# Loading w_in in two column parts between the loads of head pairs 4 and 5, holding later loads, and storing the last output in two parts

## The chip, the cores and the metric

The kernel runs on one core of a Trainium2 chip. The metric is the device time of the slowest (here the only) core in microseconds, the median of several executions. Before the change it is 290.6 us (four runs, 289.97 to 291.48). The profile shows one execution with a span of 289.0 us.

Engines in the profile: PE is TensorE, PEld its weight loads, DVE is VectorE, ACT is ScalarE, POOL is GpSimd. SPq is the queue of DMA instructions that SyncE issues.

## The reference

Block-sparse attention for 4 batches of 8 heads (768 positions, head size 64), followed by a two-matrix feed-forward layer over all 3072 tokens:

```python
# per head: scale, causal mask and a mask of at most 3 chosen key blocks of 64
k_rep = k.reshape(B, H, n_blocks, 64, D).mean(axis=3)
gate  = einsum('bhsd,bhnd->bhsn', q, k_rep)      # causal blocks only
mask  = own block, or among the 3 largest gates  # and causal by position
attn  = softmax(where(mask, 0.125 * q @ k.T, -1e9)) @ v
# all heads of a token side by side: x is [3072, 512]
h   = x @ w_in                                   # w_in  [512, 2048]
out = gelu_tanh(h) @ w_out                       # w_out [2048, 512]
```

## The kernel before

The work goes by *pairs* of heads: pair p = 4 * batch + number in the batch, 16 pairs in all. For a pair, k, q and v are loaded, k and q are turned (from pair 3 on by VectorE, 32 by 32 blocks), the gates and the mask are made ("pre"), then scores, exponentials, weighted values, normalisation and the turn of the result ("heads"). After four pairs, the batch goes through w_in (16 column blocks f of 128, with a GELU each) and w_out (6 row blocks).

A small scheduler in Python places every operation on its engines before anything is emitted. It knows estimated durations and priorities, and its result is the order of instructions *on each engine*. On the chip VectorE and ScalarE take their lists in that order, so an instruction that waits for data also delays all instructions behind it on that engine (below: 9.11 us on VectorE). The Trainium skill says so too ("Perfetto Trace Analysis", Tensor Engine Instruction): ScalarE, VectorE and GpSimd are "strict FIFO".

The parts that the change touches:

```python
    def load(p, key, at_least):
        ...
        def emit_t(_):                      # k and q from pair 3 on: four DMAs
            sd = io.tile([128, NC * 4, 32], FP32, tag=key, name=f"{key}_sd_{p}")
            for hh in range(2):
                for a in range(2):
                    nc.sync.dma_start(      # 128-byte runs
                        out=sd[64 * hh + 32 * a:64 * hh + 32 * a + 32],
                        in_=SRC[key][b, 2 * hp + hh].rearrange(
                            "(t i) (a j) -> a i t j", i=32, j=32)[a])
        ...
        go = add({SP: us}, emit_t if dve else emit,
                 [free_sd.get(...), at_least] + ..., prio=...)

    def load_w(name, dst, src, n, deps, prio):      # w_in, w_out: 2 MB in float16
        view = src.rearrange("(i p) f -> p i f", p=128)
        def emit(_):
            nc.gpsimd.dma_start(out=dst, in_=view)
        go = add({POOL: 1.3}, emit, deps, prio=prio)
        go = add({SP: 11.5}, lambda _: None, [go], prio=prio)   # plan only
        return add({"NONE": 0.0}, lambda _: None, [go], prio=prio, lag=1.9)

    # the scheduler's calls, in order (cut)
    for p in range(NPAIR):
        load(p, "k", None)
        load(p, "q", None)
        if p < HP:                                   # HP = 4
            ...
            if p == HP - 1:
                load(p, "v", None)
                w_ready["in"] = load_w("in", w_in16, moe_w_in, HP,
                                       [ld["q", p], ld["v", p]], 399)
        else:
            load(p, "v", None)
        pre(p)
        ...                                          # heads, w_out, s1(b), s2(b)

    # first feed-forward product: waits for all of w_in
    mm = add({PE: 0.324}, mm_e, [mm, xts[b][ci], exps[b][-1], w_ready["in"]], ...)
    # second: one [128, 512] output tile, one copy and one store per row block
    for ti in range(NC): ...
        def out_e(_, ti=ti):
            nc.sync.dma_start(out=out_rows[b * NC + ti], in_=T["osb", b, ti])
```

The softmax here doesn't subtract the row's maximum and nothing guards it: scores larger than these inputs give would overflow.

Of the kernel before, what the change touches and what calls it, by code (L numbers as in the profile page):

```python
# [8 lines left out]
FP32 = mybir.dt.float32  # L9
FP16 = mybir.dt.float16  # L10
# [23 lines left out]
class Plan:  # L34
# [13 lines left out]
    def add(self, *a, **kw):  # L48
        op = Op(*a, **kw)
        self.ops.append(op)  # L50
        return op
# [70 lines left out]
def kernel(  # L122
# [9 lines left out]
    nc = tc.nc  # L132
    B, H, S, D = q.shape
    NBLK = S // 64
    NC = S // 128
    DM = H * D
    DFF = moe_w_in.shape[1]
    NF = DFF // 128
    HP = H // 2
# [12 lines left out]
    hd = ctx.enter_context(tc.tile_pool(name="hd", bufs=3))  # L152
# [4 lines left out]
    obp = ctx.enter_context(tc.tile_pool(name="obp", bufs=3))  # L157
# [16 lines left out]
    w_in16 = persist.tile([128, HP, DFF], FP16)  # L174
    w_out16 = persist.tile([128, NF, DM], FP16)
# [13 lines left out]
    PE, ACT, DVE, POOL, SP = "PE", "ACT", "DVE", "POOL", "SP"  # L189
    add = plan.add  # L190
    T = {}

    def copy(eng, out, in_):
        if eng == ACT:
            nc.scalar.copy(out=out, in_=in_)
        elif eng == POOL:
            nc.gpsimd.tensor_copy(out=out, in_=in_)
        else:
            nc.vector.tensor_copy(out=out, in_=in_)
# [13 lines left out]
    def load(p, key, at_least):  # L213
        b, hp = divmod(p, HP)

        def emit(_):
            sd = (iov if key == "v" else io).tile(
                [128, NC, 2, 64], FP32, tag=key, name=f"{key}_sd_{p}")
            for hh in range(2):
                nc.sync.dma_start(  # L220
                    out=sd[:, :, hh, :],
                    in_=SRC[key][b, 2 * hp + hh].rearrange(
                        "(c p) d -> p c d", p=128))
            T[key, p] = sd
        def emit_t(_):
# [4 lines that stand above are left out]
                    nc.sync.dma_start(  # L230
# [3 lines that stand above are left out]
            T[key, p] = sd  # L234
        if p == 0 and key != "v":
            sd = T[key, p] = io.tile([128, NC, 2, 64], FP32, tag=key,
                                     name=f"{key}_sd_{p}")
            for a in range(2):
                def emit_h(_, a=a):
                    for hh in range(2):  # L240
                        nc.sync.dma_start(  # L241
                            out=sd[:, 3 * a:3 * a + 3, hh, :],
                            in_=SRC[key][b, 2 * hp + hh].rearrange(
                                "(a c p) d -> a p c d", p=128, c=3)[a])
                go = add({SP: 0.95}, emit_h, [], prio=-500)
                ld[key, p, a] = add({"NONE": 0.0}, lambda _: None, [go],
                                    prio=0, lag=1.9)
            went[key, p] = go
            return
        dve = key != "v" and by_dve(p)  # L250


        us = 2.75 if dve else 1.75
        go = add({SP: us}, emit_t if dve else emit,
                 [free_sd.get((key, p - (PV if key == "v" else PF))), at_least]
                 + ([went["k", p], went["q", p]] if key == "v" else []),
                 prio=1000 * (b - 1) + 580 + hp if b else 10 * p - 500)
        went[key, p] = go
        ld[key, p] = add({"NONE": 0.0}, lambda _: None, [go],
                         prio=1000 * b + hp, lag=1.9)  # L260
# [8 lines left out]
            [ld["v", p], old],  # L269
            prio=1000 * (b - 1) + 599 + hp if b else 100 * hp - 55)  # L270

    def load_w(name, dst, src, n, deps, prio):
        res = []
        view = src.rearrange("(i p) f -> p i f", p=128)

        def emit(_):
            nc.gpsimd.dma_start(out=dst, in_=view)
        go = add({POOL: 1.3}, emit, deps, prio=prio)

        go = add({SP: 11.5}, lambda _: None, [go], prio=prio)  # L280
        return add({"NONE": 0.0}, lambda _: None, [go], prio=prio, lag=1.9)


    c_E = {}
# [706 lines left out]
    def s1(b):  # L991
        for f in range(NF):
            mm = None
            for ci in range(HP):
                def mm_e(_, f=f, ci=ci):
                    hps = plan.buf["hps", b, f]
                    for (u, e) in ((0, 512), (512, S)):
                        nc.tensor.matmul(  # L998
                            hps[:, u:e],
                            w_in16[:, ci, f * 128:(f + 1) * 128],  # L1000
                            T["xT", b][:, ci, u:e],
                            start=(ci == 0), stop=(ci == HP - 1))
                mm = add({PE: 0.324}, mm_e,
                         [mm, xts[b][ci], exps[b][-1], w_ready["in"]],
                         1000 * b + 600 + f, takes=("wide", ("hps", b, f)))

            def ge_e(_, f=f):
                if ("gT", b) not in T:
                    T["gT", b] = gtp.tile([128, NF, S], FP16, tag="gT",
                                          name=f"gT_{b}")  # L1010
                nc.scalar.activation(  # L1011
                    out=T["gT", b][:, f, :],
                    in_=plan.buf["hps", b, f][:, 0:S],
                    func=AF.Gelu_apprx_tanh, bias=0.0, scale=1.0)
            gelus.setdefault(b, []).append(
                add({ACT: 0.7}, ge_e,
                    [mm, table(("gelu", b), exps[b], 1000 * b + 599)]
                    + s2_done.get(b - 2, []),
                    1000 * b + 600 + f, gives=[("hps", b, f)]))

    def s2(b):
        kind = "ops" if b < B - 1 else "tail"
        prev = None
        for ti in range(NC):
            mm = prev
            for f in range(NF):
                def mm_e(_, ti=ti, f=f):
                    nc.tensor.matmul(  # L1028
                        plan.buf["ops", b, ti],
                        T["gT", b][:, f, ti * 128:(ti + 1) * 128],  # L1030
                        w_out16[:, f, :],
                        start=(f == 0), stop=(f == NF - 1))
                mm = add({PE: 0.216}, mm_e,
                         [mm, gelus[b][f], w_ready["out"]],
                         1000 * b + 1580 + 0.1 * ti,
                         takes=(kind, ("ops", b, ti)))
            prev = mm

            def cp_e(eng, ti=ti):
                osb = obp.tile([128, DM], FP32, tag="osb", name=f"osb_{b}_{ti}")  # L1040
                T["osb", b, ti] = osb
                copy(eng, osb, plan.buf["ops", b, ti])
            cp = add({DVE: 0.6, ACT: 0.5}, cp_e, [mm], 1000 * b + 500,
                     gives=[("ops", b, ti)])

            def out_e(_, ti=ti):
                nc.sync.dma_start(out=out_rows[b * NC + ti],
                                  in_=T["osb", b, ti])
            add({SP: 0.9}, out_e, [cp], 1000 * b + 500)
            s2_done.setdefault(b, []).append(mm)  # L1050

# [14 lines left out]
                takes=("warm", ("warm", n)), gives=[("warm", n)])  # L1066
    consts()
    w_ready = {}
    for p in range(NPAIR):
        load(p, "k", None)  # L1070
        load(p, "q", None)
        if p < HP:
            if p:
                load(p - 1, "v", None)
                cast_v(p - 1, None)
            if p == HP - 1:
                load(p, "v", None)
                cast_v(p, None)
                w_ready["in"] = load_w("in", w_in16, moe_w_in, HP,
                                       [ld["q", p], ld["v", p]], 399)  # L1080
        else:
            load(p, "v", None)
            cast_v(p, last[p - NB]["v"])
        if p:
            pre(p)
        else:
            pre_first()
        if p < HP - 1:
            continue
        for x in range(HP) if p == HP - 1 else (p,):  # L1090
            (both_heads if x < HP else heads)(x)
        if p == HP - 1:
            w_ready["out"] = load_w("out", w_out16, moe_w_out, NF,
                                    [ld["v", 3], last[HP - 1]["n"]], 581)
        b, hp = divmod(p, HP)
        if hp == HP - 1:
            s1(b)
            s2(b)
# [35 lines left out]
```

## Time and profile before

| Part of the profiled run, 289.0 us | from to (us) |
|---|---|
| attention of batch 0 | 0 to 59.3 |
| w_in on batch 0 | 59.3 to 81.3 |
| w_out on batch 0, mixed with attention of batch 1 | 81.5 to 122.7 |
| end of w_in on batch 1 | 146.6 |
| last w_out matmul | 285.3 |

TensorE is busy 94% of the span. From the page of the kernel before, the 40 equal slices of 7.2 us; a digit is the busy share in tenths, and PEclk is the granted TensorE clock in tenths of full speed:

```profile
PE   7899952999999999999999979999999999999997
...
PEclk9999995899999999999999999999999999999999
```

Slices 6 and 7 (36 to 50 us) are the hole, and the clock falls just behind it. The table by stretch of the kernel before gives the numbers. A row is the stretch, its length, the busy time and count of each engine, then the clock, the DMA share and GB/s:

```profile
core 0: us, PE busy (x) PEld busy (x) DVE busy (x) ACT busy (x) POOL busy (x), PEclk, DMA share, GB/s
30.00:40.00 10.00, 9.94 (x137) 6.06 (x137) 6.06 (x22) 9.17 (x13) 5.20 (x12) 1.00 1.15 193
40.00:48.50 8.50, 0.04 (x1) 0.05 (x2) 1.72 (x4) 0.85 (x2) 0.09 (x1) 0.67 1.09 193
48.50:53.00 4.50, 4.50 (x42) 2.83 (x42) 2.83 (x8) 1.62 (x2) 0.02 (x1) 0.50 1.42 175
```

TensorE does nothing for 8.5 us and then works at half clock for 4.5 us. No engine computes in the hole, while the DMA column stays high. The Trainium skill ("TensorE: Matmul & The Clock Gate", Part 1) says that a TensorE left idle for a window of about 3.4 us falls to half clock and comes back after a busy window; here the clock is 0.50 after the gap, and 0.99 from 53.0 to 59.3 us.

Why it waits is read from the chain of waits of the kernel before (start, length, what). The chain is followed back from the last instruction, so each line was released by the one above it:

```profile
31.60 0.70 SPq L230
...
32.34 9.48 SPq L230
...
41.87 4.75 DMA k_sd_683<-in_k_dram
...
46.75 0.98 DVE kT_5_817 L403
...
47.84 0.57 DVE xn_755 L902
...
48.45 0.50 PE bank_91 L914 x3
```

And from VectorE's instructions in order of time (the brackets hold the idle time before, and what ended it):

```profile
36.68 0.96 DVE L403 STREAM_TRANSPOSE kT_4_803<-k_sd_516 128x768 f32<-128x768 f32 x1
46.75 0.98 DVE L403 STREAM_TRANSPOSE kT_5_817<-k_sd_683 128x768 f32<-128x768 f32 x1 [9.11 <-DMA k_sd_683<-in_k_dram]
47.65 0.16 DVE L901 RECIPROCAL zr_1_835<-bank_90 128x6 f32<-128x6 f32 x1
47.84 0.56 DVE L902 TENSOR_TENSOR xn_755<-bank_90,zr_1_835 128x384 f16<-128x384 f32 x1
```

This is the key reading. `kT_5` is the turn of pair 5's k, which belongs to batch 1; TensorE's first matmul that uses what is made of it (pair 5's gates) comes at 64.91 us. `zr_1` and `xn_755` normalise a pair of batch 0, and TensorE needs them now. They stand behind `kT_5` in VectorE's list, so they wait 9.1 us for a load that has nothing to do with them. The load is late because its third DMA issue took 9.48 us. At that time GpSimd's w_in transfer was under way: issued at 30.56 us, landed 14.3 us later.

### The profile page before, as it was taken

The page shows a single profiled execution, that of the slowest core. Times are in us where ns is not written, and L with a number is a line of the kernel's source. Part 1 is how long each engine was busy: PE and PEld are TensorE (multiplying, and loading weights), DVE is VectorE, ACT ScalarE, POOL GpSimd, SP SyncE. Part 2 cuts the span into 40 slices and gives each one's busy share as a digit, 9 for nine tenths or more (in the row PEclk, how much of TensorE's full clock was granted, in tenths as well). Part 3 has the DMA queues.
Part 4 walks back from the last instruction along what each step waited for, and adds up shares of the span by engine and source line. Part 5 has one row for each costly group of instructions (what it writes and reads, how often), then busy time and mean ns, then how long its engine had stood idle before and what let it go on. Part 6 is the DMA issues. An engine that isn't in the chain of part 4 may idle for free.

```text
span 289.0 us, 5917 instructions
## 1 busy us (share of the span) xinstructions
PE 272.6 (94%) x2304; PEld 166.7 (58%) x2304; DVE 138.7 (48%) x453; ACT 182.5 (63%) x241; POOL 46.5 (16%) x111
## 2 busy tenths in 40 slices
PE   7899952999999999999999979999999999999997
PEld 5676621756666656565656545666556644655443
DVE  6679625485628998389526991184013310000000
ACT  3568860575689998258689980176799932664111
POOL 5112420300012332000015530000034400000000
PEclk9999995899999999999999999999999999999999
DMA  5999999999805987999999921151011311000121
GB/s 135 228 156 150 190 214 174 142 186 200 130 0 119 140 147 143 214 186 152 169 145 196 134 72 73 74 71 23 0 39 30 92 41 71 36 2 0 73 75 73
DMA packets 133149, 32.44 MB, mean 112 GB/s; under 512 B 127489, under 2 KB 129537, under 8 KB 133121
## 3 DMA queue, kind: packets, MB, share of 16 engines
q1 hardware_dynamic: 130528, 27.87, 56.5%
q0 software_dynamic: 2592, 4.19, 8.1%
q8 instruction: 18, 0.29, 0.5%
q14 instruction: 11, 0.08, 0.1%
HBM read 27.26 MB, written 6.29 MB: 116 GB/s over the span
## 4 chain that ended last, share of the span: by engine, by line
PE 58%; DVE 14%; SPq 13%; DMA 6%; ACT 5%; issue 3%; DVEq 0%; ACTq 0%
PE wide_89 L998 11%; PE wide_88 L998 11%; SPq L230 10%; PE bank_90 L1028 6%; PE bank_91 L1028 5%; PE bank_93 L1028 4%; PE bank_92 L1028 4%; PE wide_88 L752 2%; DMA v_sd_1910<-in_v_dram 2%; PE wide_89 L752 2%; DMA k_sd_683<-in_k_dram 2%; SPq L220 1%; SPq L241 1%; DMA k_sd_205<-in_k_dram 1%; PE wide_89 L830 1%
## 5 line engine op out<-in xcount | busy, mean ns | idle before, releaser
L998 PEld LDWEIGHTS <-w_in_107 128*128 128x128 f16 x512 | 50.4, 103 | 30.2 <-issue 1.0
L1028 PEld LDWEIGHTS <-gT_3437 128*128 128x128 f16 x96 | 9.4, 98 | 11.2
L1063 PEld LDWEIGHTS <-zero 128*128 128x128 f16 x110 | 11.0, 111 | 5.6 <-issue 2.7
L1028 PEld LDWEIGHTS <-gT_2754 128*128 128x128 f16 x96 | 9.1, 97 | 8.2
L1028 PEld LDWEIGHTS <-gT_1940 128*128 128x128 f16 x96 | 9.1, 99 | 7.8
L1028 PEld LDWEIGHTS <-gT_1041 128*128 128x128 f16 x96 | 9.3, 103 | 6.2
L998 PE MATMUL wide_89<-xT_1480,w_in_107 128*128 128x512 f16 x64 | 12.5, 325 | 0.1
L998 PE MATMUL wide_89<-xT_2414,w_in_107 128*128 128x512 f16 x64 | 12.5, 325 | 0.0
L1028 PE MATMUL bank_90<-w_out_108,gT_1041 128*128 128x512 f16 x48 | 12.5, 379 | 0.0
L998 PE MATMUL wide_88<-xT_1480,w_in_107 128*128 128x512 f16 x64 | 12.2, 325 | 0.0
L998 PE MATMUL wide_88<-xT_2414,w_in_107 128*128 128x512 f16 x64 | 12.2, 325 | 0.0
L998 PE MATMUL wide_88<-xT_412,w_in_107 128*128 128x512 f16 x64 | 12.1, 325 | 0.0
L998 PE MATMUL wide_88<-xT_3104,w_in_107 128*128 128x512 f16 x64 | 12.0, 326 | 0.0
L998 PE MATMUL wide_89<-xT_412,w_in_107 128*128 128x512 f16 x64 | 11.8, 326 | 0.0
L998 PE MATMUL wide_89<-xT_3104,w_in_107 128*128 128x512 f16 x64 | 11.7, 326 | 0.0
L722 ACT ACT_TABLE_LOAD x8 | 10.3, 1283 | 0.9 <-PEq L1118 0.8
L1063 PE MATMUL bank_90<-zero 128*128 128x256 f16 x33 | 9.5, 294 | 1.1 <-DVE bmask L170 1.1
L1011 ACT ACTIVATE gT_1041<-wide_88 128x768 f16<-128x768 f32 x8 | 6.5, 811 | 5.1 <-PE wide_88 L998 5.1
L1028 PE MATMUL bank_92<-w_out_108,gT_2754 128*128 128x512 f16 x32 | 9.7, 380 | 0.0
L1011 ACT ACTIVATE gT_2754<-wide_88 128x768 f16<-128x768 f32 x8 | 6.5, 810 | 4.3 <-PE wide_88 L998 4.2
L1011 ACT ACTIVATE gT_1940<-wide_89 128x768 f16<-128x768 f32 x8 | 6.5, 811 | 4.0 <-PE wide_89 L998 3.9
L1011 ACT ACTIVATE gT_3437<-wide_89 128x768 f16<-128x768 f32 x8 | 6.5, 811 | 3.9 <-PE wide_89 L998 3.9
(937 smaller groups left out, 690.8 us busy)
## 6 DMA issues: line engine op xcount, KB each, us to landing
w_in_107<-in_moe_w_in_dram POOLq DMA_DIRECT2D x1, 2048.0 KB, 14.3
w_out_108<-in_moe_w_out_dram POOLq DMA_DIRECT2D x1, 2048.0 KB, 15.9
k_sd_133<-in_k_dram SPq DMA_DIRECT2D x4, 96.0 KB, 2.3
q_sd_134<-in_q_dram SPq DMA_DIRECT2D x4, 96.0 KB, 2.4
k_sd_205<-in_k_dram SPq DMA_DIRECT2D x2, 192.0 KB, 3.6
v_sd_221<-in_v_dram SPq DMA_DIRECT2D x2, 192.0 KB, 4.3
q_sd_245<-in_q_dram SPq DMA_DIRECT2D x2, 192.0 KB, 4.3
k_sd_272<-in_k_dram SPq DMA_DIRECT2D x2, 192.0 KB, 4.5
```

Source lines behind the costliest of these rows:

```text
L220: nc.sync.dma_start(out=sd[:, :, hh, :], in_=SRC[key][b, 2 * hp + hh].rearrange("(c p) d -> p c d", p=128))
L230: nc.sync.dma_start(out=sd[64 * hh + 32 * a:64 * hh + 32 * a + 32], in_=SRC[key][b, 2 * hp + hh].rearrange("(t i) (a j) -> a i t j", i=32, ...
L241: nc.sync.dma_start(out=sd[:, 3 * a:3 * a + 3, hh, :], in_=SRC[key][b, 2 * hp + hh].rearrange("(a c p) d -> a p c d", p=128, c=3)[a])
L722: nc.scalar.activation(out=t, in_=bmask[:, 0, 0:1], func=AF.Exp if key[0] == "exp" else AF.Gelu_apprx_tanh, bias=0.0, scale=1.0)
L752: nc.tensor.matmul(st[:, x:e], kT16[i][h][0:76, k0], qT16[i][h][0:76, q0], start=True, stop=True)
L830: nc.tensor.matmul(st[:, 512 * h + x + lo - q0:512 * h + x + w], (T["E2"][h] if mask else kT16[i][0])[r, j * 128:(j + 1) * 128], qT16[i][m ...
L998: nc.tensor.matmul(hps[:, u:e], w_in16[:, ci, f * 128:(f + 1) * 128], T["xT", b][:, ci, u:e], start=(ci == 0), stop=(ci == HP - 1))
L1011: nc.scalar.activation(out=T["gT", b][:, f, :], in_=plan.buf["hps", b, f][:, 0:S], func=AF.Gelu_apprx_tanh, bias=0.0, scale=1.0)
L1028: nc.tensor.matmul(plan.buf["ops", b, ti], T["gT", b][:, f, ti * 128:(ti + 1) * 128], w_out16[:, f, :], start=(f == 0), stop=(f == NF - 1))
L1063: nc.tensor.matmul(plan.buf["warm", n][:, 0:256], zero, z, start=True, stop=True)
```

## The change

The intent is to stop the batch-1 loads and w_in from getting in each other's way. The loads of pair 4 (k, q) go ahead of w_in. w_in comes in two column parts, so that the first product can start on the first. All later loads are held, in the plan and on the chip, until the first part is there; on the chip this is done by a tiny DMA on SyncE that reads one element of w_in. The last output row block is computed, copied and stored in two halves. The diff, cut:

```diff
-    def load_w(name, dst, src, n, deps, prio):
+    def load_w(dst, src, deps, prio, parts=1):
+        view = src.rearrange("(i p) f -> p i f", p=128)
+        n = view.shape[2] // parts
         res = []
+        for x in range(parts):
+            def emit(_, x=x):
+                nc.gpsimd.dma_start(out=dst[:, :, x * n:(x + 1) * n],
+                                    in_=view[:, :, x * n:(x + 1) * n])
+            go = add({POOL: 1.1}, emit, deps, prio=prio)
+            go = add({SP: 11.5 / parts}, lambda _: None, [go] + res[-1:], prio=prio)
+            res.append(go)
+        return [add({"NONE": 0.0}, lambda _: None, [go], prio=prio, lag=1.9)
+                for go in res]
+
+    def hold_loads(deps):
+        def emit(_):
+            t = hd.tile([128, 1], FP32, tag="tab", name="tab_hold")
+            nc.sync.dma_start(out=t[0:1].bitcast(FP16), in_=w_in16[0:1, 0, 0:2])
+        return add({SP: 0.05}, emit, deps, prio=-1000)
 ...
-                         [mm, xts[b][ci], exps[b][-1], w_ready["in"]],
+                         [mm, xts[b][ci], exps[b][-1], w_ready["in"][2 * f // NF]],
 ...
+        parts = [(ti, 0, DM) for ti in range(NC)]
+        if b == B - 1:                       # last output in two halves
+            parts[-1:] = [(NC - 1, x, x + DM // 2) for x in (0, DM // 2)]
 ...
     for p in range(NPAIR):
-        load(p, "k", None)
-        load(p, "q", None)
+        for key in "kq":
+            if p != HP:
+                load(p, key, held[0] if held else None)
 ...
-                w_ready["in"] = load_w("in", w_in16, moe_w_in, HP,
-                                       [ld["q", p], ld["v", p]], 399)
+                for key in "kq":
+                    load(HP, key, None)
+                w_ready["in"] = load_w(w_in16, moe_w_in,
+                                       [went["v", p], went["q", HP]], 399, 2)
+                held.append(hold_loads([w_ready["in"][0]]))
         else:
-            load(p, "v", None)
+            load(p, "v", held[0])
```

Because a scheduler decides the order, the diff does not show the main effect: in VectorE's new list, pair 5's turn comes after both normalisations of pair 3 and after pair 4's mask.

More of the change, by code (lines that the diff above doesn't have):

```diff
@@ L270, in cast_v @@
             prio=1000 * (b - 1) + 599 + hp if b else 100 * hp - 55)
-    def load_w(name, dst, src, n, deps, prio):
+    def load_w(dst, src, deps, prio, parts=1):
+        view = src.rearrange("(i p) f -> p i f", p=128)
+        n = view.shape[2] // parts
         res = []
-        view = src.rearrange("(i p) f -> p i f", p=128)
+        for x in range(parts):
[3 more added lines that the diff above has]
+            go = add({POOL: 1.1}, emit, deps, prio=prio)
+            go = add({SP: 11.5 / parts}, lambda _: None, [go] + res[-1:],
+                     prio=prio)
+            res.append(go)
+        return [add({"NONE": 0.0}, lambda _: None, [go], prio=prio, lag=1.9)
+                for go in res]
+    def hold_loads(deps):
         def emit(_):
-            nc.gpsimd.dma_start(out=dst, in_=view)
-        go = add({POOL: 1.3}, emit, deps, prio=prio)
-        go = add({SP: 11.5}, lambda _: None, [go], prio=prio)
-        return add({"NONE": 0.0}, lambda _: None, [go], prio=prio, lag=1.9)
+            t = hd.tile([128, 1], FP32, tag="tab", name="tab_hold")
+            nc.sync.dma_start(out=t[0:1].bitcast(FP16),
+                              in_=w_in16[0:1, 0, 0:2])
+        return add({SP: 0.05}, emit, deps, prio=-1000)
     c_E = {}
@@ L1023, in s2, with mm_e, cp_e, out_e @@
         prev = None
-        for ti in range(NC):
+        parts = [(ti, 0, DM) for ti in range(NC)]
+        if b == B - 1:
+            parts[-1:] = [(NC - 1, x, x + DM // 2) for x in (0, DM // 2)]
+        for n, (ti, x0, x1) in enumerate(parts):
             mm = prev
             for f in range(NF):
-                def mm_e(_, ti=ti, f=f):
+                def mm_e(_, n=n, ti=ti, x0=x0, x1=x1, f=f):
                     nc.tensor.matmul(
-                        plan.buf["ops", b, ti],
+                        plan.buf["ops", b, n][:, 0:x1 - x0],
                         T["gT", b][:, f, ti * 128:(ti + 1) * 128],
-                        w_out16[:, f, :],
+                        w_out16[:, f, x0:x1],
                         start=(f == 0), stop=(f == NF - 1))
-                mm = add({PE: 0.216}, mm_e,
-                         [mm, gelus[b][f], w_ready["out"]],
+                mm = add({PE: 0.216 * (x1 - x0) / 512}, mm_e,
+                         [mm, gelus[b][f], w_ready["out"][0]],
                          1000 * b + 1580 + 0.1 * ti,
-                         takes=(kind, ("ops", b, ti)))
+                         takes=(kind, ("ops", b, n)))
             prev = mm
-            def cp_e(eng, ti=ti):
-                osb = obp.tile([128, DM], FP32, tag="osb", name=f"osb_{b}_{ti}")
-                T["osb", b, ti] = osb
-                copy(eng, osb, plan.buf["ops", b, ti])
-            cp = add({DVE: 0.6, ACT: 0.5}, cp_e, [mm], 1000 * b + 500,
-                     gives=[("ops", b, ti)])
-            def out_e(_, ti=ti):
-                nc.sync.dma_start(out=out_rows[b * NC + ti],
-                                  in_=T["osb", b, ti])
+            def cp_e(eng, n=n, x0=x0, x1=x1):
+                osb = obp.tile([128, DM], FP32, tag="osb", name=f"osb_{b}_{n}")
+                T["osb", b, n] = osb
+                copy(eng, osb[:, x0:x1], plan.buf["ops", b, n][:, 0:x1 - x0])
+            cp = add({DVE: 0.6, ACT: 0.5} if x1 - x0 == DM else
+                     {DVE: 0.33, ACT: 0.36}, cp_e, [mm], 1000 * b + 500,
+                     gives=[("ops", b, n)])
+            def out_e(_, n=n, ti=ti, x0=x0, x1=x1):
+                nc.sync.dma_start(out=out_rows[b * NC + ti][:, x0:x1],
+                                  in_=T["osb", b, n][:, x0:x1])
             add({SP: 0.9}, out_e, [cp], 1000 * b + 500)
@@ L1068 @@
     w_ready = {}
+    held = []
     for p in range(NPAIR):
-        load(p, "k", None)
-        load(p, "q", None)
+        for key in "kq":
+            if p != HP:
+                load(p, key, held[0] if held else None)
         if p < HP:
@@ L1092 @@
         if p == HP - 1:
-            w_ready["out"] = load_w("out", w_out16, moe_w_out, NF,
+            w_ready["out"] = load_w(w_out16, moe_w_out,
                                     [ld["v", 3], last[HP - 1]["n"]], 581)
```

## The prediction

> **What bounds it now.** TensorE is busy 94% of the 289.0 us span (busy table), with one hole: from 40.0 to 48.5 us it is busy 0.04 us of 8.5, and from 48.5 to 53.0 us its granted clock is 0.50 (table by stretch). The chain of waits passes through the hole: SyncE's queue is stuck 9.48 us on the third of four small loads of pair 5's k (32.34 to 41.8 us), 4.75 us more until the fourth has landed, then VectorE's transpose of that k (0.98 us), then the normalisation of pair 3, which TensorE needs. The list of waits gives VectorE 9.1 us on that load. The queue is stuck because of w_in: 2 MB issued at 30.56 us, 14.3 us to landing. k7 beside w_out (9.07 us for four issues instead of about 3) shows the same. The Trainium skill ("DMA: Bandwidth & Descriptors", Queues, rings and completion order) says each engine takes turns between queues packet by packet; this agrees, k's runs being 128 bytes and w_in's kilobytes. So an in-order VectorE waits for data wanted later and holds up work wanted now.
>
> **What the change does.** The scheduler is told that pair 5's loads come after w_in's first half, so pair 5's k transpose moves behind both normalisations of pair 3 and the mask work of pair 4 (instruction order). Pair 3's remaining units, 40.0 to 59.3 us before, need roughly 7 us by the pace of pair 2. Part 1 should land near 40 us (half of 14.3 from about 32), part 2 near 47. The first w_in matmuls come at about 46 us, four of the 16 columns ahead of pair 4's mask. At the end of the first w_in stage (81.2 us before) 12 to 14 us should be won.
>
> Part is given back. The held loads (v4, k5, q5, k6, v5, q6, k7) start near 41 us beside part 2 and then w_out, issued near 45 instead of 55.35; before, most had a quiet gap from 43 to 55 us. At the rate seen beside w_out (about six issues in 15 us) they end near 72 to 75 us. That uses slack: before, SyncE's queue then waited 12.6 us for the first output. Pair 5's gates moved to the end of the w_in stage, so I expect stalls of 1 to 2 us. Afterwards loads, ScalarE and VectorE set the pace to about 130 us (queue nearly full from 89 to 126), and loads come only 7 to 10 us earlier. From 160 us on everything shifts. Extra: one tiny load, one weight issue (about 1 us of GpSimd), 16 matmuls.
>
> Last output in halves: a 0.59 us copy and a 2 us store follow the last matmul; half of each saves about 0.3 us.
>
> **Sum.** 10 us from the hole and the slow clock: 281.0 us, range 276.0 to 287.0. Chances: faster by over 2% 0.83, within 2% 0.14, slower 0.03.
>
> **What shows it.** No TensorE gap over 2 us from 40 to 49 us, clock 1.0; VectorE's wait for pair 5's k no longer ahead of pair 3's normalisation; w_in matmuls from about 46 us, column 16 done near 68; TensorE's busy total equal or a few us lower; the tail shorter by 0.3 us.
>
> **What would make it wrong.** Held loads starved by part 2 and w_out, so TensorE stops at pair 5's or 6's gates (new hole at 60 to 80 us); ScalarE blocked by the cast of v4, placed after the second GELU; a load-bound second batch that hands the gain back by 130 us.

## The result, and the profile after

The changed kernel takes 280.9 us (median of four runs, 280.27 to 285.32, of which the 285.32 is slow). Executions over 1.5% slower than the fastest of the same kernel are left out of the means. The ratio of fast runs to fast runs of before is 0.9656, 95% interval 0.9614 to 0.9698. Ratios here are the mean time of one kernel's fast runs over that of the other's in the same rounds, so not quite the ratio of the medians quoted. The profiled span is 278.6 us against 289.0.

From the page of the changed kernel, TensorE's 40 slices of 7.0 us. There is no PEclk line, because the clock was full throughout:

```profile
PE   7899999999999988999999979999999999999998
```

The table by stretch of the changed kernel, same columns:

```profile
40.00:48.50 8.50, 8.50 (x105) 6.40 (x102) 5.16 (x29) 5.91 (x9) 2.30 (x4) 1.00 1.06 182
48.50:53.00 4.50, 4.50 (x36) 3.10 (x34) 1.69 (x7) 3.97 (x6) 0.00 (x0) 1.00 1.24 180
```

Where TensorE was idle it is now busy all 8.5 us. VectorE in the changed kernel, in order of time:

```profile
36.14 0.96 DVE L417 STREAM_TRANSPOSE kT_4_794<-k_sd_516 128x768 f32<-128x768 f32 x1
...
39.23 0.18 DVE L915 RECIPROCAL zr_1_848<-bank_90 128x6 f32<-128x6 f32 x1
39.45 0.56 DVE L916 TENSOR_TENSOR xn_749<-bank_90,zr_1_848 128x384 f16<-128x384 f32 x1
...
52.05 0.49 DVE L199 COPY qT_1_110<-bank_93 12x640 f16<-12x640 f16 x1
61.12 0.98 DVE L417 STREAM_TRANSPOSE kT_5_1138<-k_sd_1094 128x768 f32<-128x768 f32 x1 [8.58 <-DMA k_sd_1094<-in_k_dram]
```

VectorE *still* waits 8.6 us for pair 5's k. Only the place of the wait has changed: nothing urgent stands behind it. The normalisation ends at 40.0 us instead of 48.4. SyncE's queue in the changed kernel (an issue's length is how long it held the queue) shows that the small loads still crawl, now beside part 2 and w_out:

```profile
40.33 0.74 SPq L293 DMA_DIRECT2D tab_hold<-w_in_107  x1
41.17 0.98 SPq L220 DMA_DIRECT2D v_sd_955<-in_v_dram  x2
42.25 8.25 SPq L230 DMA_DIRECT2D k_sd_1094<-in_k_dram  x4
50.60 10.49 SPq L230 DMA_DIRECT2D q_sd_1119<-in_q_dram  x4
61.19 2.18 SPq L230 DMA_DIRECT2D k_sd_1145<-in_k_dram  x4
```

The gain by milestone, in us of the profiled runs, read from the TensorE matmuls in order of time:

| Milestone | before | after | won |
|---|---|---|---|
| first w_in matmul | 59.3 | 43.6 | 15.7 |
| end of w_in on batch 0 | 81.3 | 68.1 | 13.2 |
| end of w_in on batch 1 | 146.6 | 136.9 | 9.7 |
| last w_out matmul | 285.3 | 275.1 | 10.2 |
| span | 289.0 | 278.6 | 10.4 |

13.2 us are won by the end of the first w_in stage, and about 3.5 us of it are lost again before the second one ends. From there on all stages just shift. The loss lies in the first w_out stage, which is mixed with batch 1's attention. Its row in the table by stretch, first before, then after:

```profile
81.30:122.70 41.40, 41.31 (x399) 25.40 (x396) 29.93 (x77) 34.16 (x44) 9.90 (x24) 1.00 0.75 133
```

```profile
68.10:113.10 45.00, 42.71 (x414) 26.43 (x412) 37.42 (x110) 36.12 (x46) 10.08 (x24) 1.00 0.90 160
```

The stage is 3.6 us longer: TensorE works 1.4 us more in it (work that the kernel before does elsewhere) and is idle 2.3 us instead of 0.1. Nearly all of that idle time is one wait of 2.13 us, from 103.2 to 105.3 us. VectorE in order of time, and then the chain of waits, show what it waits for:

```profile
104.10 0.56 DVE L199 CAST v_119<-v_sd_1732 128x768 f16<-128x768 f32 x1 [3.22 <-DMA v_sd_1732<-in_v_dram]
104.58 0.68 DVE L199 COPY osb_3_1808<-bank_91 128x512 f32<-128x512 f32 x1
```

```profile
99.02 5.06 DMA v_sd_1732<-in_v_dram
...
104.10 0.56 DVE v_119 L199
104.66 0.61 DVE osb_3_1808 L199
...
105.31 3.61 PE bank_91 L1046 x16
```

VectorE stands 3.22 us before the cast of pair 9's v, and behind that cast stands the copy of an output tile out of `bank_91`, the bank that TensorE writes next. It is the pattern of the old hole again, smaller and in another place.

### The profile page after: what moved, and what is told of

It reads as the page before. It is cut to its first block, busy times and chain, and to the rows that moved or that the text cites. A ratio compares the mean times of both kernels' runs of the same rounds, so it can differ in the third digit from the quotient of the medians.

```text
span 278.6 us, 5963 instructions
## 1 busy us (share of the span) xinstructions
PE 269.8 (97%) x2320; PEld 166.8 (60%) x2320; DVE 139.5 (50%) x455; ACT 182.0 (65%) x240; POOL 46.9 (17%) x112
## 3 DMA queue, kind: packets, MB, share of 16 engines
q1 hardware_dynamic: 130676, 27.87, 57.5%
## 4 chain that ended last, share of the span: by engine, by line
PE 69%; DVE 9%; SPq 8%; DMA 6%; ACT 4%; issue 2%; POOL 1%; DVEq 0%; ACTq 0%
PE wide_89 L1012 14%; PE wide_88 L1012 14%; PE bank_92 L1046 7%; PE bank_93 L1046 6%; PE bank_91 L1046 6%; SPq L220 4%; PE bank_90 L1046 3%; SPq L230 3%; PE wide_88 L766 2%; DMA q_sd_329<-in_q_dram 2%; PE wide_89 L766 2%; DMA v_sd_1732<-in_v_dram 2%; PE wide_89 L844 1%; SPq L241 1%; PE bank_91 L516 1%
## 5 line engine op out<-in xcount | busy, mean ns | idle before, releaser
L1012 PEld LDWEIGHTS <-w_in_107 128*128 128x128 f16 x512 | 50.3, 102 | 29.5 <-issue 0.3
L1046 PEld LDWEIGHTS <-gT_3434 128*128 128x128 f16 x112 | 10.9, 98 | 9.9
L1046 PEld LDWEIGHTS <-gT_984 128*128 128x128 f16 x96 | 9.0, 101 | 8.6 <-issue 2.3
L1046 PEld LDWEIGHTS <-gT_2751 128*128 128x128 f16 x96 | 9.1, 97 | 8.2
L1046 PEld LDWEIGHTS <-gT_1935 128*128 128x128 f16 x96 | 9.1, 99 | 7.8
L1012 PE MATMUL wide_88<-xT_1475,w_in_107 128*128 128x512 f16 x64 | 12.3, 325 | 0.2 <-ACT gT_1935 L1025 0.2
L1012 PE MATMUL wide_89<-xT_412,w_in_107 128*128 128x512 f16 x64 | 12.3, 326 | 0.0
L1082 PE MATMUL bank_90<-zero 128*128 128x256 f16 x36 | 10.2, 285 | 1.2 <-DVE bmask L170 1.1
L1025 ACT ACTIVATE gT_2751<-wide_88 128x768 f16<-128x768 f32 x8 | 6.5, 809 | 4.3 <-PE wide_88 L1012 4.2
L1025 ACT ACTIVATE gT_984<-wide_88 128x768 f16<-128x768 f32 x8 | 6.5, 808 | 4.0 <-PE wide_88 L1012 4.0
L1025 ACT ACTIVATE gT_3434<-wide_89 128x768 f16<-128x768 f32 x8 | 6.5, 811 | 3.9 <-PE wide_89 L1012 3.9
```

What stands on the lines that cost most here:

```text
L1012: nc.tensor.matmul(hps[:, u:e], w_in16[:, ci, f * 128:(f + 1) * 128], T["xT", b][:, ci, u:e], start=(ci == 0), stop=(ci == HP - 1))
L1025: nc.scalar.activation(out=T["gT", b][:, f, :], in_=plan.buf["hps", b, f][:, 0:S], func=AF.Gelu_apprx_tanh, bias=0.0, scale=1.0)
L1046: nc.tensor.matmul(plan.buf["ops", b, n][:, 0:x1 - x0], T["gT", b][:, f, ti * 128:(ti + 1) * 128], w_out16[:, f, x0:x1], start=(f == 0), s ...
L1082: nc.tensor.matmul(plan.buf["warm", n][:, 0:256], zero, z, start=True, stop=True)
```

## The experiments

Twelve runs on the chip, in three calls; kernels of one call share the runs of the kernel before (medians 291.24, 290.69 and 290.12 us). "Correct" means equal to the reference within tolerance. Theory A says that the gain is the order on VectorE: pair 5's turn no longer stands in front of urgent work. Theory B says that it is keeping the small loads away from w_in, and theory C that it is starting on half of w_in.

### b_order: the kernel before, only the plan changed

```diff
-        load(p, "k", None)
-        load(p, "q", None)
+        late = w_ready["in"] if p > HP else None      # plan only, no wait on the chip
+        load(p, "k", late)
+        load(p, "q", late)
 ...
-            load(p, "v", None)
+            load(p, "v", w_ready["in"])
```

> The kernel before, with one thing told to the scheduler alone: all loads of pair 5 and later, and v of pair 4, are planned after w_in. No wait is added on the chip, w_in stays in one part, the output in one. Theory A (the in-order VectorE stood in front of pair 5's k; putting that transpose behind pair 3's normalisations is the gain): about 282 us, 279.5 to 284.5, TensorE's gap at 40 to 49 us gone, clock 1.0 there, although SyncE's queue still sticks 8 to 10 us on pair 5's k. Theory B (the gain comes from keeping the small loads away from w_in): 288 to 292. Theory C (the gain comes from starting on half of w_in): 286 to 291.

Measured: correct, 281.19 us median (fast runs 280.89 to 281.2, one slow run of 291.8), ratio 0.9646 (0.9592 to 0.9699). The SyncE queue of this run, in order of time:

```profile
31.92 14.46 SPq L230 DMA_DIRECT2D k_sd<-in_k_dram  x4
46.48 10.03 SPq L230 DMA_DIRECT2D q_sd<-in_q_dram  x4
```

and its table by stretch:

```profile
40.00:48.50 8.50, 8.50 (x110) 6.39 (x107) 4.29 (x21) 6.25 (x9) 2.83 (x6) 1.00 0.97 161
```

The queue sticks on pair 5's k for 14.5 us, longer even than in the kernel before, and TensorE is busy through the whole former hole. One hint to the scheduler, with no wait, no split and no second output half, brings nearly all of the gain. Theory A holds here; B and C fall as main causes.

### b_hold: the kernel before, only the wait on the chip added

```diff
             sd = io.tile([128, NC * 4, 32], FP32, tag=key, name=f"{key}_sd_{p}")
+            if (key, p) == ("k", HP + 1):       # in emit_t, ahead of the four DMAs
+                t = hd.tile([128, 1], FP32, tag="tab", name="tab_hold")
+                nc.sync.dma_start(out=t[0:1].bitcast(FP16), in_=w_in16[0:1, 0, 0:2])
```

> The kernel before with its plan untouched, every engine's order as it was, and one addition: SyncE waits for all of w_in (a tiny read of it) before it issues pair 5's k. Theory A: slower, 292 to 296 us, because pair 5's k lands about 3 us later (near 50 us instead of 46.6) and VectorE stands in front of it all the longer; TensorE's gap grows from 8.5 to 11 or 12 us. Theory B: faster, under 287, because w_in lands earlier.

Measured: correct, 293.08 us median (292.64 to 293.63), ratio 1.0054 (1.0010 to 1.0099). VectorE in order of time:

```profile
50.89 0.98 DVE L407 STREAM_TRANSPOSE kT<-k_sd 128x768 f32<-128x768 f32 x1 [12.52 <-DMA k_sd<-in_k_dram]
```

Pair 5's k is used 4.1 us later than before (50.89 against 46.75), and TensorE's gap grows from 8.5 to 11.86 us. The wait on the chip without the new order makes the kernel slower (0.5%, just clear of noise). Theory B, that keeping these loads away from w_in is by itself the gain, is refuted.

### a_no_hold: the changed kernel without the wait on the chip

```diff
         def emit(_):
-            t = hd.tile([128, 1], FP32, tag="tab", name="tab_hold")
-            nc.sync.dma_start(out=t[0:1].bitcast(FP16), in_=w_in16[0:1, 0, 0:2])
+            pass
```

> The changed kernel without the wait on the chip: its plan, order and split are kept, only the tiny read of w_in that held SyncE's queue is taken out, so v4 and pair 5's k are issued from about 31 us and stick in the queue beside w_in. Theory A: 279.5 to 283 us, the same within 1.5 us; part 1 lands 1 to 3 us later, pair 5's k and q earlier. If late loads are what gives back the 3.6 us between 81 and 123 us, it is rather at the low end or below. Theory B: over 286.

Measured: correct, 279.87 us median (279.77 to 280.16), ratio 0.9605 (0.9564 to 0.9646). w_in's first part landed 10.2 us after its issue instead of 9.5. The wait on the chip is not needed, and the median is about 1 us below that of the changed kernel. They were run at other times. The intervals of their ratios overlap; and when the changed kernel was run again (`after_again`, below), its full-clock runs took 279.62 to 280.05 us, the same as here. A benefit of leaving it out is not shown.

### a_one_part: the changed kernel with w_in in one part

```diff
-                w_ready["in"] = load_w(w_in16, moe_w_in, [...], 399, 2)
+                w_ready["in"] = load_w(w_in16, moe_w_in, [...], 399, 1)
 ...
-                         [mm, ..., w_ready["in"][2 * f // NF]],
+                         [mm, ..., w_ready["in"][0]],
```

> The changed kernel with w_in in one part: planned so, SyncE held until all of it is there (about 45 us instead of 40), the output still in two parts. Theory A: 280.5 to 284 us, the first w_in matmuls at 44 to 48 us, held loads about 4 us later. Theory C (half of w_in is what starts the stage early): 285 or more.

Measured: correct, 281.89 us median (280.92 to 282.35), ratio 0.9664 (0.9617 to 0.9711). The first w_in matmul comes at 48.4 us instead of 43.6 and that stage ends at 70.6 instead of 68.1. Part of this is not the split: this profiled run has a half clock from 11.3 to 15 us, before the change acts, and its normalisations at 15 to 27 us, early in batch 0, are already 1.5 to 1.9 us late. The Trainium skill ("Perfetto Trace Analysis", DMA Optimizations) says that splitting a DMA may let some work start sooner; it does so here, by some 3 us once that delay is taken off. At the end the medians differ by about 1 us (281.89 against 280.9 and 280.65), which is within the spread. Theory C is refuted as the main cause.

### after_again and a_one_out: is the last output in halves worth anything?

`after_again` is the changed kernel as it is. `a_one_out` undoes the halves:

```diff
-        if b == B - 1:
+        if False:
             parts[-1:] = [(NC - 1, x, x + DM // 2) for x in (0, DM // 2)]
```

> The changed kernel as it is, run again so that the three others of this call have it on their own chip. 280.3 to 281.3 us in its fast runs.

> The changed kernel with its last output in one part, all else kept. If the two halves save what was predicted (half of the 0.59 us copy and something of the store), it is 0.2 to 0.5 us slower than the changed kernel, 280.8 to 281.6 us, and the time from the last w_out matmul to the end of the span grows by as much. If the halves do nothing: within 0.1 us.

Measured, both correct and in five rounds: 280.65 us (279.62 to 282.02, ratio 0.9662, 0.9627 to 0.9697) and 280.77 us (280.02 to 282.23, ratio 0.9669, 0.9636 to 0.9703). The difference of 0.12 us is below the spread. At equal clock (three runs of each, means) it is 0.34 us at 1.000 and 0.10 us at 0.994, and the ranges overlap. So the expected 0.2 us or more is neither shown nor excluded by the times. From the profiles, in order of time: the last copy of the changed kernel, and the last copy of the kernel with one part:

```profile
276.89 0.42 DVE L199 COPY osb<-bank 128x256 f32<-128x256 f32 x1 [1.32 <-PE bank L1046]
```

```profile
276.99 0.58 ACT L195 COPY osb<-bank 128x512 f32<-128x512 f32 x1 [2.87 <-PE bank L1046]
```

Half the copy, on VectorE, is 0.16 us shorter than the whole one on ScalarE, not half as long, and the span behind the copy's end is 3.0 us in one and 2.9 us in the other, so the smaller store gains nothing that shows. From the last matmul to the end it is 3.5 us with the halves and 3.6 us without. `after_again` also fell partly outside what was on record (280.3 to 281.3): three of its six runs had a clock of 1.000 and 279.6 to 280.1 us, three a clock of 0.994 and 281.3 to 282.0 us. All count as fast. The profiled run is one of clock 0.994, and its trace shows where the time goes:

```profile
105.08 5.30 PE L1046 MATMUL bank<-w_out,gT 128*128 128x512 f16 x16 [1.76 <-DVE osb L199]
```

Behind the same wait for VectorE's copy as in the first profile, the clock is 0.66 from 105 to 110 us, and these 16 matmuls take 5.30 us instead of 3.61. Why the clock falls there in this run and stays full in the first one, behind a longer wait (2.13 us), no run shows.

### b_light_in: is it w_in's traffic that sticks the queue?

A wrong result: the kernel before, with a sixteenth of w_in.

```diff
-            nc.gpsimd.dma_start(out=dst, in_=view)
+            if name == "in":
+                nc.gpsimd.dma_start(out=dst[:, :, 0:128], in_=view[:, :, 0:128])
+            else: ...
-                            w_in16[:, ci, f * 128:(f + 1) * 128],
+                            w_in16[:, ci, 0:128],
```

> Wrong result on purpose: the kernel before with one sixteenth of w_in loaded and used sixteen times, every engine's order kept. If w_in's traffic is what sticks SyncE's queue and so makes the gap: pair 5's k is issued in about 3 us instead of 12, VectorE does not wait for it, TensorE's gap at 40 to 48.5 us is gone and the clock stays at 1.0; 279 to 282.5 us. If the gap has another cause (a buffer that comes free late, the order alone): 288 us or more.

Measured: 280.86 us median (280.37 to 281.16), ratio 0.9679 (0.9653 to 0.9706). SyncE's queue and VectorE, each in order of time:

```profile
30.93 3.37 SPq L230 DMA_DIRECT2D k_sd<-in_k_dram  x4
```

```profile
38.76 0.98 DVE L406 STREAM_TRANSPOSE kT<-k_sd 128x768 f32<-128x768 f32 x1 [1.40 <-DMA k_sd<-in_k_dram]
```

With the order untouched and w_in's bytes gone, pair 5's k is issued in 3.4 us instead of 12.3, VectorE waits 1.4 us instead of 9.1, and TensorE's gap is 0.8 us. So two things together make the hole: the traffic of w_in, and an order that puts an urgent normalisation behind a load stuck in that traffic. Removing either is enough. This run also sizes the hole and the slow clock by themselves: the end of w_in on batch 0 comes at 71.8 us instead of 81.3, so 9.5 us, and the span shrinks by 9.6.

### a_light_out: are the loads beside w_out what gives gain back?

A wrong result: the changed kernel with a sixteenth of w_out.

```diff
-            w_ready["out"] = load_w(w_out16, moe_w_out, ...)
+            w_ready["out"] = load_w(w_out16[:, 0:1], moe_w_out[0:128], ...)
-                        w_out16[:, f, x0:x1],
+                        w_out16[:, 0, x0:x1],
```

> Wrong result on purpose: the changed kernel with only one sixteenth of w_out loaded and used sixteen times, so that nearly all of w_out's traffic is gone, with every engine's order kept. Theory A1 (of the 13.2 us won by the end of the first w_in stage, about 3 are given back because the held loads crawl beside w_out): the queue's 10.5 us for pair 5's q shrinks to about 3, all loads up to pair 7 come some 8 to 10 us earlier, and the time is 277 to 279 us. Theory A2 (given back because the loads of pairs 7 to 9 stand in SyncE's order behind output stores and buffers that come free late): 279.7 to 281 us, with the same 1.5 to 2 us wait of TensorE near 105 us.

Measured: 280.47 us median (279.9 to 282.02), ratio 0.9659 (0.9622 to 0.9697), against 0.9662 of the changed kernel in the same call: no difference. Pair 5's q now needs 2.89 us of the queue instead of 10.49, and pair 7's k is issued at 57.5 us instead of 67.9, yet nothing is faster. Theory A1 is refuted. VectorE in order of time shows why early data does not help:

```profile
57.73 0.98 DVE L417 STREAM_TRANSPOSE kT<-k_sd 128x768 f32<-128x768 f32 x1
69.53 0.28 DVE L527 TENSOR_TENSOR gm<-bank,cgate 128x120 f32<-128x120 f32 x1 [10.82 <-PE bank L516]
```

VectorE runs out of work at 58.7 us and waits 10.8 us for pair 5's gates, which stand at the end of the w_in stage in TensorE's list. The scheduler put them there because it believed that w_out would block the queue. (TensorE's wait near 105 us, for a copy behind pair 9's v, is still there, with 1.23 us instead of 2.13.)

### a_light_plan: and if the plan knows that the loads come early?

As above, and the scheduler is told that w_out takes the queue 0.1 us:

```diff
-            go = add({SP: 11.5 / parts}, lambda _: None, [go] + res[-1:], prio=prio)
+            go = add({SP: us / parts}, ...)          # us = 0.1 for w_out
```

> Wrong result on purpose: as the run with a sixteenth of w_out, but the scheduler is told too that w_out takes the queue 0.1 us instead of 11.5, so that the gates of pairs 5 and 6 are planned inside the first w_in stage. Theory A3 (3 to 4 us are given back after 68 us because the order leaves VectorE idle before pair 5's gates, which stand at the end of the first w_in stage, and its mask work of pairs 5 to 7 comes on top of the next stage; the loads themselves are not the limit): VectorE is busy 14 us or more in the w_in stage instead of 11, the first w_out stage ends 2 to 4 us earlier, 276.5 to 279 us. If A3 is wrong: 279.7 to 281 us as without the plan.

Measured: 278.75 us median (278.42 to 278.94), ratio 0.9610 (0.9582 to 0.9639). The tables by stretch of `a_light_out` for its first w_in stage, and then of this run for about the same 24 us (its own stage ends at 73.4 us, because work of batch 1 is mixed in):

```profile
43.90:68.40 24.50, 24.50 (x175) 15.99 (x175) 11.02 (x36) 16.56 (x22) 1.11 (x3) 1.00 0.87 119
```

```profile
43.70:68.00 24.30, 23.67 (x174) 15.36 (x172) 18.10 (x67) 18.67 (x26) 1.01 (x3) 1.00 1.15 158
```

VectorE (the third busy value) does 18.1 us of work in that stretch instead of 11.0, and w_in on batch 1 ends at 134.9 us instead of 136.5. The time is what theory A3 expected, but that it is won by VectorE's earlier work is not shown. TensorE is idle 1.6 us between 43.7 us and the end of w_in on batch 1, against 1.7 us in `a_light_out`, so no waiting is saved there. The difference is later: from 140 to 180 us TensorE is idle 0.3 us instead of 1.7, because `a_light_out` waits 1.66 us for a normalisation just before 162.8 us and this run does not. The plan changed in other places too (some w_out matmuls moved up). So the run shows only that a plan which knows of the early loads is 1.6 us faster.

### n_out_pool: outputs of the first three batches from GpSimd, without the wait

```diff
-                nc.sync.dma_start(out=out_rows[...], in_=T["osb", b, n][...])
-            add({SP: 0.9}, out_e, [cp], 1000 * b + 500)
+                eng = nc.gpsimd if b < B - 1 else nc.sync
+                eng.dma_start(out=out_rows[...], in_=T["osb", b, n][...])
+            add({POOL: 1.1} if b < B - 1 else {SP: 0.9}, out_e, [cp], 1000 * b + 500)
```

> A try at something better: the changed kernel without the wait on the chip, and with the outputs of the first three batches issued by GpSimd instead of SyncE, so that no load waits in SyncE's order behind an output. Theory A2: 276.5 to 279 us, with the loads of pairs 7 to 9 earlier than 89 to 98 us. Theory A1, or GpSimd's issue cost of about 1 us each standing in front of the causal selects: 279.5 to 283 us.

Measured: correct, 282.76 us median (282.37 to 285.28), ratio 0.9758 (0.9709 to 0.9807), so 1% slower than the changed kernel. The loads of batch 1 did come about 3 us earlier (pair 9's v at 94.75 us instead of 98.40), and w_in on batch 1 still ended at 137.8 us. TensorE's wait of 2.13 us near 105 us is gone, but waits of 1.08, 1.00 and 1.19 us stand elsewhere (ending at 118.8, 121.6 and 146.5 us). Theory A2, that loads behind output stores are the limit, finds no support in the time; the plan moved everywhere, so it is not refuted by this run alone. The Trainium skill ("Perfetto Trace Analysis", DMA Optimizations) suggests one engine for input DMAs and another for output; here it did not pay.

### t_late_q and t_late_q_nh: w_out issued after pair 5's q has landed

An attempt to use the finding in a right version: the plan then puts pair 5's gates in the middle of the first w_in stage.

```diff
+                if after is not None:                # after = ("q", 5), for w_out
+                    t = hd.tile([128, 1], FP32, tag="tab", name="tab_w")
+                    nc.gpsimd.tensor_copy(out=t[0:1], in_=T[after][0:1, 0, 0:1])
                 nc.gpsimd.dma_start(out=dst[...], in_=view[...])
```

`t_late_q_nh` has the wait for w_in's first part taken out as well.

> A right version that uses A3: the changed kernel with w_out issued only after pair 5's q has landed (GpSimd reads one element of it first), and the scheduler told so; the gates of pair 5 then stand in the middle of the first w_in stage. Theory A3: w_out lands near 66 us, just before it is needed at 69 us; the first w_out stage ends 1 to 3 us earlier; 277.5 to 280 us. Rival: the first w_out matmul has to wait for w_out, or the loads of pairs 6 and 7 crawl instead: 280.5 to 284 us.

> The same late w_out without the wait on the chip that holds SyncE for w_in's first part. Pair 5's q lands about as early (near 51 us), so the same as with the wait within 1 us: 277.5 to 280 us if A3 holds.

Measured, both correct: 291.15 us (289.98 to 293.05, ratio 1.0042, 0.9991 to 1.0093) and 291.49 us (291.3 to 292.15, ratio 1.0051, 1.0024 to 1.0079). All of the gain is gone, as the rival said it might, and by more than it said. ScalarE of `t_late_q` in order of time, and then TensorE:

```profile
57.57 0.81 ACT L1029 ACTIVATE gT<-wide 128x768 f16<-128x768 f32 x1
63.98 0.83 ACT L195 CAST kT<-kT 64x768 f16<-64x768 f32 x1 [5.60 <-DVE kT L421]
64.72 0.80 ACT L1029 ACTIVATE gT<-wide 128x768 f16<-128x768 f32 x1
69.70 0.83 ACT L195 CAST v<-v_sd 128x768 f16<-128x768 f32 x1 [4.19 <-DMA v_sd<-in_v_dram]
```

```profile
65.57 1.68 PE L1016 MATMUL wide<-xT,w_in 128*128 128x512 f16 x6 [4.66 <-ACT gT L1029]
...
71.30 2.72 PE L1016 MATMUL wide<-xT,w_in 128*128 128x512 f16 x8 [2.88 <-ACT gT L1029]
```

It is the same illness in another engine. w_out, now issued at 51.3 us, sticks the loads of pair 6's k and pair 5's v. Their casts stand between two GELUs in ScalarE's list, the GELUs wait behind them, and TensorE waits for the GELUs: two gaps of 4.7 and 2.9 us. Behind them the clock is 0.55 (65.5 to 70.3 us) and 0.50 (70.3 to 75.0 us), and the w_in stage ends at 81.8 us instead of 68.1. No version tried that gives the right result is clearly better than the changed kernel.

### What the runs say together

| Profiled run | w_in on batch 0 ends | w_in on batch 1 ends | span |
|---|---|---|---|
| before | 81.3 | 146.6 | 289.0 |
| b_hold | 84.7 | 149.6 | 291.9 |
| b_light_in (wrong result) | 71.8 | 137.1 | 279.4 |
| b_order | 69.4 | 137.4 | 279.5 |
| a_no_hold | 68.5 | 137.1 | 278.5 |
| a_one_part | 70.6 | 138.4 | 280.6 |
| after | 68.1 | 136.9 | 278.6 |
| a_light_out (wrong result) | 68.4 | 136.5 | 278.2 |
| a_light_plan (wrong result) | 73.4 | 134.9 | 276.7 |
| t_late_q | 81.8 | 147.4 | 291.4 |

The profiled run of `a_one_part` is one of clock 0.994. Without the hole, the second w_in stage ends near 137 us however early the first one ended (68.1 to 71.8 us). What the new order wins beyond the 9.5 us of the hole is therefore lost again. `b_light_in`, which keeps the old order, loses nothing between the two stages (65.3 us from end to end, as before), so the loss belongs to the new order. Only the plan of `a_light_plan` gets below 136.

## Why the prediction was right

The time (280.9 us against 281.0), the direction and the main term were right. That the time fits to 0.1 us is partly luck, as the last points show. Point by point:

- **What bounds it: right.** The hole, the stuck queue, and VectorE standing in front of pair 5's k were the cause. `b_light_in` and `b_order` show it from two sides.
- **What the order does: right.** No TensorE gap and a full clock where the hole was. `b_order` shows that this step alone brings the gain.
- **Where w_in lands: right to about 1.5 us.** Part 1 landed at 40.3 us (predicted about 40), part 2 at 45.5 (predicted about 47). The first w_in matmul came at 43.6 us (predicted about 46), 2.4 us early.
- **End of the first w_in stage: right.** 68.1 us (predicted near 68), 13.2 us won (predicted 12 to 14).
- **The sum: right, in part by luck.** "10 us from the hole and the slow clock". Measured alone by `b_light_in` it is 9.5 us at that point and 9.6 at the end. But the way to it, 12 to 14 us won and so 2 to 4 us given back again, needed a loss that came for another reason than the predicted one.
- **Stalls at pair 5's gates of 1 to 2 us: wrong.** There is no TensorE wait over 0.3 us in that stage. The held loads were issued by 70.7 us, a little earlier than the predicted 72 to 75.
- **Why part is given back: wrong in its cause.** The size was about right (13.2 down to 10), but it was put down to loads crawling beside w_out. `a_light_out` takes that traffic away and gains nothing. By the trace, the first w_out stage loses 2.2 us by idle time of TensorE, nearly all of it the wait of 2.13 us behind pair 9's v, and 1.4 us by work that moved into the stage. This is read from the trace and not tested by taking that wait away alone. A plan that knows of early loads gains 1.6 us (`a_light_plan`), through a later wait.
- **0.3 us from the last output in halves: not confirmed.** The time from the last matmul to the end of the span went from 3.7 to 3.5 us (289.0 minus 285.3, 278.6 minus 275.1), and the run without it is slower by 0.12 us, within noise. The mis-sized term by the traces is "half of each": the half copy takes 0.42 us instead of 0.59, and the store is no shorter.

Two parts of the change are thus not needed for the gain: the wait on the chip (`a_no_hold`) and the output halves (`a_one_out`). The split of w_in is worth about 1 us by the medians, which is within the spread.

## What to carry to other kernels

When an engine's list is fixed at build time, ask for every instruction that waits on a load what stands behind it, and order it by when its data can really come and not by when it would be nice to have. Tell the scheduler about a large transfer before adding waits on the chip: the hint that gained 3.5% here needed no instruction at all, and the wait without the hint cost 0.5%. When a stage is won early, look for the next stage that does not follow, and test each suspect by taking it away, because in `t_late_q` moving a large transfer only moved the place where something urgent stood behind it.

## What the Trainium skill lacked or had wrong

- "DMA: Bandwidth & Descriptors", Queues, rings and completion order, says that the engines take turns between queues by packets, but not how little that leaves to a queue of 128-byte runs beside one of large rows, nor that the issuing instruction is held meanwhile. Here one 96 KB issue took 9.48 us beside w_in, and four together 14.46 us in `b_order`, against mostly 2.2 to 3.8 us for four without such a neighbour.
- "Perfetto Trace Analysis", DMA Instruction — HWDGE, says that an issue's profiled window is lock wait, descriptor generation and semaphore push, and not data movement. It does not say that the window grows with other traffic. Here its length followed that of the other queue: 12.25 us with w_in, 3.37 us with a sixteenth of it, for the same instructions.
- "Perfetto Trace Analysis", DMA Optimizations, offers an engine for inputs and another for outputs. It gives no sign of when it costs: with the outputs of three batches on GpSimd, and a plan that moved with them, the kernel was 1% slower (282.76 against 280.65 us).
- No page that was read says that a transfer not yet needed can stop TensorE through an in-order engine in between, although "strict FIFO" is stated. It cost 8.5 us of idle and 4.5 us at half clock here, 2.1 us more in the changed kernel, and 7.5 us in `t_late_q`.
- "TensorE: Matmul & The Clock Gate", Part 1, agrees with the 0.50 seen behind the gap. The mean clock of 0.994 in half the runs of one kernel goes with 1.2 to 2.4 us more time (279.6 to 280.1 against 281.3 to 282.0 us). In the one that was profiled, the low clock (0.66 from 105 to 110 us) stands behind a gap of only 1.76 us, while the first profile keeps 1.00 behind 2.13 us. What decides this is shown by no run here.
